# Two-layer transformer block: five of 21 pairs of score maxima per block as halves of 256 keys, in a new order of sixteen key tiles

## The chip, the cores and the metric

The kernel runs on one core of one Trainium2 chip. The metric is the device time of one execution in microseconds. Before the change it is 3515.99 us, the median of three runs (3515.44 to 3516.27).

## The reference

Two rounds of the same pair of layers: attention with 32 heads of 20 elements over 2048 positions, then a dense layer with a squared ReLU. All of it is float32.

```
qkv = (x @ wqkv).reshape(B, S, 3, H, Dh)...      # B=1, S=2048, D=640, H=32, Dh=20
scores = einsum("bhqd,bhkd->bhqk", q, k) * Dh ** -0.5
o = einsum("bhqk,bhkd->bhqd", softmax(scores), v) ... @ wo
...
x = x + A(layernorm(x));  x = x + B(layernorm(x))      # B: relu(x @ w1 + b1)**2 @ w2 + b2
x = x + A(layernorm(x));  x = x + B(layernorm(x))      # the same weights again
```

The softmax subtracts the maximum of each row of scores, so the kernel needs each row's maximum over all 2048 keys before it may compute an exponential.

## The kernel before, in words

Each layer is a projection stage (queries, keys, values), an attention sweep, and the dense layer. The change is in the sweep.

**Blocks.** A block is four heads (a group g of eight) and 512 queries (one of four). There are 32 blocks per layer. The four heads lie as two pairs p; within a pair the even head's operands are on partitions 0 to 59 or 61 and the odd head's on partitions 64 and up. A product of an even head uses the upper half of TensorE's rows, one of an odd head the lower half, so one of each can run at the same time. I call these the two lanes.

**One key tile** (128 keys) of a block takes three kinds of work:

- `score` (L795 before, L832 after): keys by queries, 128x512 into one PSUM bank, four per key tile (two pairs, two heads). ScalarE takes the exponential (`exps`, L805 before, L842 after) into a tile e.
- `pv` (L810 before, L847 after): the value step, e times the values of four heads, added up in bank 7 over sixteen key tiles. It uses all rows of the array.
- `smax` (L701 for the product, L712 for the reduction before; L715 and L726 after): queries by keys, 128 queries by 512 keys of one head into one bank, and a VectorE reduction to one maximum per query. This is for a block that comes up later; the maxima of a block go into one small tile mx, from which `mrows_max` makes the negative maxima that are loaded as two further rows of the queries.

**What sets the order.** The program is written out by hand: `attention` runs through the string ORDER_OF_BLOCK over and over, and `op` issues what a letter stands for. One pass over the string is sixteen key tiles. `a` and `b` are the next score of the even and of the odd head with its exponential, `S` is both at once in two neighbouring banks with one exponential of 1024 columns, `m` and `n` are a whole maximum of the even and of the odd head, and `V` is the value step. The letters between two V are one run of products. When all maxima are done, LAST_ORDER takes over, which the change leaves alone.

**Banks.** Seven of the eight PSUM banks serve scores and maxima. The class Clock keeps a model of the engines while the program is written and gives each product the bank that its model says is free first. Its numbers decide which bank a product takes, and so which earlier reader it waits for; they take no part in the run.

**Waits.** A matmul is a weight load and a product on TensorE; a wait stands on the weight load. Completions of TensorE's matmuls are counted in one count. Where a matmul has to wait for another of TensorE's own, the kernel puts a step (`nc.tensor.nop`) on TensorE's queue that waits for that count, and makes the matmul wait for the step. Today this is in `Halves.catch` (L406), in the projections, where the matmul waited for is nineteen back.

Of the kernel before, what the change touches and what calls it, by code (L numbers as in the profile page):

```python
# [16 lines left out]
P = 128  # L17
# [8 lines left out]
QB = 512  # L26
# [15 lines left out]
def tile_layers(  # L42
# [22 lines left out]
    def name(p):  # L65
        n_alloc[0] += 1
        return f"{p}{n_alloc[0]}"
# [506 lines left out]
    class Clock:  # L574


        def __init__(self):
            self.free = [600 * ((b - ps_q.n - 1) % 5 - 5) for b in range(5)] + [0, 0]
            self.lane, self.over, self.fresh, self.place = [0, 0], [0, 0], [False, False], 9
            self.now, self.load, self.values, self.since = 0, 0, False, 0  # L580
            self.act, self.act_end, self.dve = 0, 0, 0
            self.ready, self.used, self.acc = {}, [], 0

        def row(self, par, b):
            s = self.now + 3
            if self.values:
                s = self.now + 542
                self.values, self.fresh, self.place = False, [True, True], 0
                self.lane, self.over, self.since = [0, 0], [0, 0], None
            s = max(s, self.lane[par], self.load)  # L590
            w = max(s - 116, self.free[b] + 34)
            t = max(s, w + 61)
            more = max(0, w + 116 - t)
            if self.since is None:
                self.since = t
            self.now = t
            self.load = 0 if w + 177 < t else w + 116 + (46 if t > s + 10 else 0)
            self.lane[par] = t + 232 + more
            if self.fresh[par]:
                self.fresh[par] = False  # L600
                self.lane[par] = max(self.lane[par], self.since + 338)
            self.over[par] = t + more
            self.place += 1
            return t + more + {1: 532, 2: 563, 3: 465}.get(self.place, 433)

        def first(self):
            return min(range(7), key=self.free.__getitem__)

        def score(self, par, kt):
            b = self.first()  # L610
# [7 lines left out]
            return banks[:, b, :]  # L618

        def both(self, kt):  # L620
            b = min(range(6), key=lambda b: max(self.free[b : b + 2]))
# [87 lines left out]
    def smax(dst, t, p, sub, c, par):  # L709

        by_queries(dst, t, p, sub, c, par)
        nc.vector.tensor_reduce(  # L712
            maxima(t)[:, 2 * p + par, sub, c : c + 1], dst, axis=AX.X, op=ALU.max
        )

    def pair_of(t, p, sub, c):
# [6 lines left out]
    def smax_two(t, p, sub, c):  # L723

        for par, dst in enumerate(pair_of(t, p, sub, c)):
            nc.vector.tensor_reduce(  # L726
                maxima(t)[:, 2 * p + par, sub, c : c + 1], dst, axis=AX.X, op=ALU.max
            )

    def step_two(t, p, sub, x):  # L730
# [6 lines left out]
    def both_two(t, p, sub, x, r):  # L737

        c = 2 * "de".index(x)
        for par, dst in enumerate(pair_of(t, p, sub, c)):  # L740
            nc.vector.tensor_tensor_reduce(  # L741
                out=r[par],
                in0=dst,
                in1=r[par],
                scale=1.0,
                scalar=LEAST,
                op0=ALU.add,
                op1=ALU.max,
                accum_out=maxima(t)[:, 2 * p + par, sub, c : c + 1],
            )  # L750

    PAIRS = [(p, sub) for p in range(2) for sub in range(4)]
# [161 lines left out]
        [(0, 0, "d"), (0, 1, "d")],  # L914
        [(1, 0, "d"), (1, 1, "d"), (2, 0, "d"), (2, 1, "d")],
    ]
    PARTLY = {g * NQB + qb for x in DOUBLE for g, qb, c in x}

# [27 lines left out]
    def qkv(first, x_src, rest, lead):  # L946
# [204 lines left out]
    def attention(first, x_src, first_rows):  # L1151
# [1 line left out]
        es_of = {}  # L1153
        e_n.clear()
        weights.extend(slot([P, 2, QB], F32, "e") for _ in range(6))
        st_n, sm_n = [0, 0], [0, 0]
        state = {"begun": -1, "done": 0, "acc": None, "debt": 0}
        clock = Clock()
        todo = [
# [13 lines left out]
        ends = {x[0]: n for n, x in enumerate(todo)}  # L1173
        blocks = sorted(ends)
        firsts = {todo[0][0]: 0, **{t: ends[s] + 1 for s, t in zip(blocks, blocks[1:])}}
        over = {t for t in range(NBLK) if t not in ends and t not in done}
        rows = {"next": min(t for t in range(NBLK) if t not in done), "at": None}

        def begin(i):
# [27 lines left out]
            if i in split:  # L1207
                split.pop(i)()

        def op(o):  # L1210
            if o in "abS":
                pars = (0, 1) if o == "S" else ("ab".index(o),)
                i, p = divmod(st_n[pars[0]], 2)
                assert len(pars) == 1 or st_n[0] == st_n[1]
                if i >= last:
                    return
                if i > state["begun"]:
                    state["begun"] = i
                    begin(i)
                es = es_of.setdefault(i, {})  # L1220
                dst = clock.both(i) if o == "S" else clock.score(pars[0], i)
                for par in pars:
                    st_n[par] += 1
                    score(
                        dst[:, par, :] if o == "S" else dst,
                        i // NKT, i % NKT, 2 * p + par, es,
                    )
                exps(es[p] if o == "S" else es[p][:, pars[0], :], dst)
            elif o in "mn":
                par = "mn".index(o)  # L1230
                n = sm_n[par]
                if n == len(todo):
                    return
                t, p, sub, c = todo[n]
                if n == firsts[t] and par == 0:
                    for s in blocks[blocks.index(t) :][:2]:
                        if s not in q_t:
                            load_q(s)
                if (t // NQB, c) not in k_t or t not in q_t:
                    return  # L1240
                sm_n[par] += 1
                smax(clock.most(par), t, p, sub, c, par)
                if n == ends[t] and min(sm_n) > n:
                    over.add(t)
                    if t * NKT > state["begun"] + 2 * NKT:
                        del q_t[t]
# [24 lines left out]
            op(o)  # L1271
            yield
        while state["done"] < last:
            for o in LAST_ORDER if min(sm_n) == len(todo) else ORDER_OF_BLOCK:
                op(o)
        assert min(sm_n) == len(todo)
        q_t.clear()
        k_t.clear()
        v_t.clear()
# [451 lines left out]
```

## Time and profile before

| | |
|---|---|
| median of three runs | 3515.99 us |
| profiled execution, its own time | 3517.9 us |
| its span from first to last instruction | 3516.1 us |
| TensorE busy | 3504.1 us |
| ScalarE (ACT) busy | 2733.7 us |
| VectorE (DVE) busy | 2732.5 us |
| granted TensorE clock | 0.999 |

The page gives busy time per engine; PE is TensorE's products, PEld its weight loads, which run beside products. Ends of matmuls are modelled, so their starts carry more than their lengths. The groups of instructions give busy time and mean duration of one, then the idle time before them and who ended it.

### The profile page before, as it was taken

What the parts mean: (1) busy time and instruction counts of PE and PEld (TensorE: products, weight loads), DVE (VectorE), ACT (ScalarE), POOL (GpSimd) and SP (SyncE); (2) the same over time, 40 slices, a digit from 0 to 9 for tenths busy, and PEclk for the clock granted to TensorE, in tenths of its full rate; (3) what the DMA queues carried; (4) which work ended last, traced back from release to release, by engine and by line L of the source; (5) the groups of instructions that cost most, each with busy time, mean ns of one, the idle gap of its engine ahead of it and who ended that gap; (6) DMA issues with size and microseconds to landing.
All of it is one profiled execution on the core that took longest, in us unless ns stands there. A gap on an engine that the chain in (4) does not pass through costs nothing.

```text
span 3516.1 us, 71077 instructions
## 1 busy us (share of the span) xinstructions
PE 3504.1 (100%) x25292; PEld 2112.9 (60%) x25292; DVE 2732.5 (78%) x5326; ACT 2733.7 (78%) x4804; POOL 828.0 (24%) x975
## 2 busy tenths in 40 slices
PE   9999999999999999999999999999999999999999
PEld 8998333333333335989989983333333333358899
DVE  8999888888888882566869988888888888825667
ACT  5888999999999996123348889999999999951233
POOL 4430334443112111120143201121221212111200
PEclk9999999999999999999999999999999999999999
DMA  7766454444222135856656652222222121358574
GB/s 259 234 207 188 143 170 134 135 126 133 60 55 60 42 103 192 310 198 237 234 195 224 194 180 69 77 76 57 77 76 55 53 58 50 103 196 308 195 253 141
DMA packets 325378, 514.87 MB, mean 146 GB/s; under 512 B 74532, under 2 KB 149796, under 8 KB 325024
## 3 DMA queue, kind: packets, MB, share of 16 engines
q1 hardware_dynamic: 324496, 508.62, 45.5%
q8 instruction: 201, 3.29, 0.4%
q10 hardware_dynamic: 528, 1.70, 0.2%
q14 instruction: 153, 1.25, 0.1%
HBM read 326.95 MB, written 183.21 MB: 145 GB/s over the span
## 4 chain that ended last, share of the span: by engine, by line
PE 96%; DMA 2%; ACT 1%; POOL 0%; DVE 0%; issue 0%; SPq 0%; POOLq 0%; ACTq 0%; DVEq 0%
PE banks L810 28%; PE banks L795 18%; PE banks L701 18%; PE banks L376 13%; PE banks L1455 9%; PE banks L396 6%; PE banks L408 5%; PE banks L391 0%; PE banks L508 0%; ACT e L805 0%; DMA x<-d_x 0%; DMA x<-in_A_x_dram 0%; SPq L78 0%; DMA few<-d_s 0%; DMA o<-d_r 0%
## 5 line engine op out<-in xcount | busy, mean ns | idle before, releaser
L805 ACT ACTIVATE e<-banks 128x512 f32<-128x512 f32 (+1 forms) x3416 | 2035.1, 691 | 56.3 <-PE banks L795 21.5
L712 DVE TENSOR_REDUCE mx<-banks 128x1 f32<-128x512 f32 x2560 | 1620.3, 685 | 321.6 <-PE banks L701 274.4
L810 PE MATMUL banks<-e,vg 128*32 128x512 f32 x8192 | 1093.5, 605 | 2.2 <-ACT e L805 2.1
L701 PE MATMUL banks<-k,q 60*128 60x512 f32 x3360 | 1060.1, 411 | 0.9 <-DMA q<-d_qk 0.9
L795 PE MATMUL banks<-q,k 62*128 62x512 f32 x4096 | 1049.0, 441 | 1.2 <-ACT v L472 0.6
L795 PEld LDWEIGHTS banks<-q,k 62*128 62x128 f32 x4096 | 514.6, 184 | 748.5 <-ACT e L805 440.9
L701 PEld LDWEIGHTS banks<-k,q 60*128 60x128 f32 x3360 | 568.0, 185 | 196.4 <-ACT e L805 64.2
L741 DVE CUSTOM_DVE_ANT_0 rl<-banks,rl 128x512 f32<-128x512 f32 x736 | 477.0, 689 | 31.1 <-PE banks L701 6.7
L734 ACT ACTIVATE rl<-banks 128x512 f32<-128x512 f32 x736 | 399.7, 602 | 57.0 <-PE banks L701 46.5
L810 PEld LDWEIGHTS banks<-e,vg 128*32 128x32 f32 x8192 | 162.2, 108 | 353.5 <-issue 270.6
L408 PE MATMUL banks<-xnT,wqk 64*128 64x512 f32 x1080 | 327.7, 393 | 0.0
L376 PE MATMUL banks<-xnT,w 128*128 128x512 f32 x1440 | 327.0, 389 | 0.0
L396 PE MATMUL banks<-xnT,wqk 64*128 64x512 f32 x1080 | 326.9, 395 | 0.0
L376 PEld LDWEIGHTS banks<-xnT,w 128*128 128x128 f32 x1440 | 270.2, 188 | 56.0
L1361 ACT ACTIVATE r<-banks,b_t 128x512 f32<-128x512 f32 x96 | 66.2, 690 | 222.1 <-PE banks L376 205.1
L854 POOL TENSOR_TENSOR few<-few,minus_t 128x16 f32<-128x16 f32 x62 | 179.9, 2902 | 239.4 <-DMA few<-d_s 234.4
L701 PE MATMUL banks<-kd,q 60*128 60x512 f32 x736 | 210.1, 398 | 0.8 <-ACT rl L734 0.6
L408 PEld LDWEIGHTS banks<-xnT,wqk 64*128 64x128 f32 x1080 | 202.1, 188 | 8.5
L396 PEld LDWEIGHTS banks<-xnT,wqk 64*128 64x128 f32 x1080 | 200.3, 187 | 11.1 <-issue 1.7
L865 POOL TENSOR_TENSOR o<-o 128x512 f32<-128x512 f32 x62 | 79.6, 1284 | 508.6 <-DMA o<-d_r 285.5
L308 POOL CAST mr<-nt 128x32 fp32r<-128x32 f32 x64 | 13.5, 212 | 775.9 <-DVE nt L767 775.9
L396 PE MATMUL banks<-wv,xnT 64*128 64x320 f32 x960 | 193.5, 308 | 0.0
(130 smaller groups left out, 3295.5 us busy)
## 6 DMA issues: line engine op xcount, KB each, us to landing
q<-d_qk SPq DMA_DIRECT2D x876, 80.0 KB
d_qk<-ev SPq DMA_DIRECT2D x80, 512.0 KB
k<-d_qk SPq DMA_DIRECT2D x444, 80.0 KB
x<-d_x SPq DMA_DIRECT2D x96, 320.0 KB
w<-d_w SPq DMA_DIRECT2D x60, 480.0 KB
d_h<-r SPq DMA_DIRECT2D x48, 512.0 KB
r<-d_h SPq DMA_DIRECT2D x48, 512.0 KB
d_o<-ot SPq DMA_DIRECT2D x248, 80.0 KB
```

The source lines that it names most:

```text
L376: nc.tensor.matmul(dst, a, b, start=(n == 0), stop=(n == last))
L396: top = nc.tensor.matmul(dst, a[:64], b[:64], start=start, stop=last)
L408: low = nc.tensor.matmul(dst, a, b, start=False, stop=last, skip_group_check=True)
L701: nc.tensor.matmul(dst, q_t[t][b : b + 60, p, sub * P : (sub + 1) * P], k_t[t // NQB, c][b : b + 60, p, :], start=True, stop=True,)
L712: nc.vector.tensor_reduce(maxima(t)[:, 2 * p + par, sub, c : c + 1], dst, axis=AX.X, op=ALU.max)
L734: nc.scalar.activation(r, dst, AF.Relu)
L741: nc.vector.tensor_tensor_reduce(out=r[par], in0=dst, in1=r[par], scale=1.0, scalar=LEAST, op0=ALU.add, op1=ALU.max, accum_out=maxima(t)[: ...
L795: nc.tensor.matmul(dst, k_t[t // NQB, kt // 4][b : b + 62, p, (kt % 4) * P : (kt % 4 + 1) * P], q_t[t][b : b + 62, p, :], start=True, stop ...
L805: nc.scalar.activation(dst, src, AF.Exp, scale=SCALE)
L810: nc.tensor.matmul(acc[32 * h : 32 * h + 32, :], v_t[t // NQB, kt // 8][:, kt % 8, 32 * h : 32 * h + 32], es[p][:, par, :], start=(kt == 0 ...
L854: nc.gpsimd.tensor_tensor(few, few, minus_t, op=ALU.pow)
L1455: nc.tensor.matmul(dst, a, b, start=first and not more, stop=last, skip_group_check=more)
```

## The change

Five of the 21 pairs of maxima in a pass are taken as halves. A pair is a block's 128 queries and 512 keys for the even and the odd head of a pair p: before, two whole products into two banks and two reductions. In halves it is taken twice, each time 256 keys for both heads: the first product (`h` for the even head first, `i` for the odd head first) opens a bank and fills one half of its columns, and later `j` fills the other half with the other head. Then one VectorE reduction (`most_of_halves`, L746) takes both maxima from that bank. So five pairs are twenty products of 256 keys and ten reductions in place of ten products of 512 keys and ten reductions. Between `h` or `i` and `j` stands a step on TensorE's queue that waits for the first half, because both write one bank from different lanes.

The string of letters is new: ten openings by `h` or `i`, each with its `j`, one more `S` with one `a` and one `b` fewer, and another order. The runs, between two `V`:

```
before: (m)bbanna bamnabm nabmnab Snanbm nambabm Sbmna Snabm SnSm bmamnS bmanban anabmbm bambann bmabanm Smban Snabm SnSm
after:  bhanmjS Sbmna SnSm bhmnajba bhmnajab hbmnajab ainmbjS SnmS ainabjmb aibSjan mbmbna bhmnajba bhmnajab nhabajmb Smban SSnm
```

Each mx tile holds eight maxima per query where it held four (a slot for each half), and is set to the least number before it is used. The list of maxima to take is shared by whole and half pairs (`taken`), and a block is done when all of its products are counted (`less`).

```diff
+        def row(self, par, b, cut=0, after=0):
+            s = max(self.now + 3, after)
...
-            self.lane[par] = t + 232 + more
+            self.lane[par] = t + 232 + more - cut
...
+        def half(self, par):
+            self.opened = self.first()
+            self.later = self.row(par, self.opened, 106) + 110
+            return banks[:, self.opened, :]
+
+        def other(self, par):
+            b = self.opened
+            t = max(self.row(par, b, 106, self.later), self.dve)
+            self.opened = None
+            self.dve, self.free[b] = t + 610, t + 698
...
-            mx_t[t] = small.tile([P, 4, 4, 4], F32, tag="mx", bufs=14, name=name("mx"))
-            if t in PARTLY:
-                nc.vector.memset(mx_t[t], LEAST)
+            mx_t[t] = small.tile([P, 4, 4, 8], F32, tag="mx", bufs=14, name=name("mx"))
+            nc.vector.memset(mx_t[t], LEAST)
...
+    def half_scores(dst, t, p, sub, c, half, par):
+
+        b = 64 * par
+        w = QB // 2
+        return nc.tensor.matmul(
+            dst[:, par * w : (par + 1) * w],
+            q_t[t][b : b + 60, p, sub * P : (sub + 1) * P],
+            k_t[t // NQB, c][b : b + 60, p, half * w : (half + 1) * w],
+            start=True,
+            stop=True,
+            skip_group_check=True,
+        )
+
+    def most_of_halves(dst, t, p, sub, c, half):
+
+        n = 2 * c + half
+        nc.vector.tensor_reduce(
+            maxima(t)[:, 2 * p : 2 * p + 2, sub, n : n + 1],
+            dst.rearrange("p (a c) -> p a c", a=2),
+            axis=AX.X,
+            op=ALU.max,
         )
...
     ORDER_OF_BLOCK = (
-        "bbannaVbamnabmVnabmnabVSnanbmVnambabmVSbmnaVSnabmVSnSmVbmamnSVbmanbanVan"
-        "abmbmVbambannVbmabanmVSmbanVSnabmVSnSmVm"
+        "bhanmjSVSbmnaVSnSmVbhmnajbaVbhmnajabVhbmnajabVainmbjSVSnmSVai"
+        "nabjmbVaibSjanVmbmbnaVbhmnajbaVbhmnajabVnhabajmbVSmbanVSSnmV"
     )
...
+            elif o in "hi":
+                if not parted:
+                    x = taken()
+                    if x is None:
+                        return
+                    parted.extend([(*x, 0), (*x, 1)])
+                x, par = parted.pop(0), "hi".index(o)
+                dst = clock.half(par)
+                opened.append((x, par, dst, half_scores(dst, *x, par)))
+            elif o == "j":
+                if not opened:
+                    return
+                x, par, dst, one = opened.pop()
+                clock.other(1 - par)
+                step = nc.tensor.nop()
+                tc.add_manual_dep(step.ins, one.ins.name, SYNC)
+                two = half_scores(dst, *x, 1 - par)
+                tc.add_manual_dep(two.ins, step.ins.name, SYNC)
+                most_of_halves(dst, *x)
+                less(x[0])
```

Two places on TensorE's queue show what moves. The first is a run of seven products in the sweep, before the change: L701 is a whole maximum, L795 a score, L810 the value step that closes the run. DVE and Activation in brackets are the readers that have to leave a bank first.

```order
L701 MATMUL banks<-k_1180,q_12667 128x512
L795 MATMUL banks<-q_12530,k_5404 128x512 [waits DVE_49]
L795 MATMUL banks<-q_12530,k_5404 128x512 [waits Activation_49]
L795 MATMUL banks<-q_12530,k_5404 128x512
L701 MATMUL banks<-k_1180,q_12667 128x512 [waits DVE_49]
L701 MATMUL banks<-k_1180,q_12667 128x512 [waits Activation_49]
L795 MATMUL banks<-q_12530,k_5404 128x512
L810 MATMUL banks<-e_5359,vg_11921 32x512 [waits DVE_49]
```

In letters this is mbbanna: three products of even heads and four of odd heads, none of which waits for another of TensorE's own.

A run of the changed kernel in the sweep, bhmnajba; L832 is a score, L715 a whole maximum, L734 a half, L847 the value step.

```order
L832 MATMUL banks<-q_14290,k_5516 128x512
L734 MATMUL banks<-k_4970,q_14087 128x256 [waits DVE_49]
L715 MATMUL banks<-k_4979,q_14087 128x512 [waits Activation_49]
L715 MATMUL banks<-k_4979,q_14087 128x512
L832 MATMUL banks<-q_14290,k_5516 128x512 [waits DVE_49]
L734 MATMUL banks<-k_4970,q_14087 128x256 [waits PE_49,PE_sequencer_49]
L832 MATMUL banks<-q_14290,k_5516 128x512 [waits Activation_49]
L832 MATMUL banks<-q_14290,k_5516 128x512
L847 MATMUL banks<-e_5355,vg_13645 32x512 x2
```

Each lane now has three whole products and one half. The second half waits for TensorE's own count (PE) through the step on its queue (PE_sequencer), three products after the first half, and two whole products stand behind it. The first half has a whole product ahead of it.

The second place is the one run of a pass, hbmnajab, in which the half stands ahead of everything else.

```order
L734 MATMUL banks<-k_4979,q_14087 128x256 [waits Activation_49]
L832 MATMUL banks<-q_14290,k_5516 128x512 [waits DVE_49]
L715 MATMUL banks<-k_4979,q_14087 128x512 [waits Activation_49]
L715 MATMUL banks<-k_4979,q_14087 128x512 [waits DVE_49]
L832 MATMUL banks<-q_14290,k_5516 128x512 [waits Activation_49]
L734 MATMUL banks<-k_4979,q_14087 128x256 [waits PE_49,PE_sequencer_49]
L832 MATMUL banks<-q_14290,k_5516 128x512 [waits DVE_49]
```

Here the first half is the run's first product, and four products stand between it and the second half.

More of the change, by code (lines that the diff above doesn't have):

```diff
@@ L582, in __init__ @@
             self.ready, self.used, self.acc = {}, [], 0
-        def row(self, par, b):
-            s = self.now + 3
+            self.opened, self.later = None, 0
+        def row(self, par, b, cut=0, after=0):
+            s = max(self.now + 3, after)
             if self.values:
-                s = self.now + 542
+                s = max(self.now + 542, after)
                 self.values, self.fresh, self.place = False, [True, True], 0
@@ L597, in row @@
             self.load = 0 if w + 177 < t else w + 116 + (46 if t > s + 10 else 0)
-            self.lane[par] = t + 232 + more
+            self.lane[par] = t + 232 + more - cut
             if self.fresh[par]:
                 self.fresh[par] = False
-                self.lane[par] = max(self.lane[par], self.since + 338)
+                self.lane[par] = max(self.lane[par], self.since + 338 - cut)
             self.over[par] = t + more
             self.place += 1
-            return t + more + {1: 532, 2: 563, 3: 465}.get(self.place, 433)
+            return t + more + {1: 532, 2: 563, 3: 465}.get(self.place, 433) - cut
         def first(self):
-            return min(range(7), key=self.free.__getitem__)
+            return min((b for b in range(7) if b != self.opened), key=self.free.__getitem__)
         def score(self, par, kt):
@@ L620, in both @@
         def both(self, kt):
-            b = min(range(6), key=lambda b: max(self.free[b : b + 2]))
+            b = min(
+                (b for b in range(6) if self.opened not in (b, b + 1)),
+                key=lambda b: max(self.free[b : b + 2]),
+            )
             t = max(self.row(par, b + par) for par in range(2))
@@ L712, in smax @@
         nc.vector.tensor_reduce(
-            maxima(t)[:, 2 * p + par, sub, c : c + 1], dst, axis=AX.X, op=ALU.max
+            maxima(t)[:, 2 * p + par, sub, 2 * c : 2 * c + 1], dst, axis=AX.X, op=ALU.max
+        )
+    def half_scores(dst, t, p, sub, c, half, par):
[8 more added lines that the diff above has]
+            skip_group_check=True,
+        )
+    def most_of_halves(dst, t, p, sub, c, half):
[5 more added lines that the diff above has]
+            op=ALU.max,
         )
@@ L726, in smax_two @@
             nc.vector.tensor_reduce(
-                maxima(t)[:, 2 * p + par, sub, c : c + 1], dst, axis=AX.X, op=ALU.max
+                maxima(t)[:, 2 * p + par, sub, 2 * c : 2 * c + 1], dst, axis=AX.X, op=ALU.max
             )
@@ L748, in both_two @@
                 op1=ALU.max,
-                accum_out=maxima(t)[:, 2 * p + par, sub, c : c + 1],
+                accum_out=maxima(t)[:, 2 * p + par, sub, 2 * c : 2 * c + 1],
             )
@@ L1155, in attention @@
         weights.extend(slot([P, 2, QB], F32, "e") for _ in range(6))
-        st_n, sm_n = [0, 0], [0, 0]
+        st_n = [0, 0]
+        whole, sm_n, parted, opened = [], [0, 0], [], []
         state = {"begun": -1, "done": 0, "acc": None, "debt": 0}
@@ L1172, in attention @@
             loads[at] = lambda qb=qb: heads(nc.sync, qb, 4)
[L1173 to L1176, printed above, removed]
+        todo.reverse()
+        undone = {}
+        for x in todo:
+            undone[x[0]] = undone.get(x[0], 0) + 2
+        blocks, begun = sorted(undone), set()
+        over = {t for t in range(NBLK) if t not in undone and t not in done}
         rows = {"next": min(t for t in range(NBLK) if t not in done), "at": None}
@@ L1208, in begin, with taken, less @@
                 split.pop(i)()
+        def taken():
+            if not todo:
+                return None
+            t, p, sub, c = todo[-1]
+            if t not in begun:
+                begun.add(t)
+                for s in blocks[blocks.index(t) :][:2]:
+                    if s not in q_t:
+                        load_q(s)
+            if (t // NQB, c) not in k_t or t not in q_t:
+                return None
+            return todo.pop()
+        def less(t):
+            undone[t] -= 1
+            if undone[t] == 0:
+                over.add(t)
+                if t * NKT > state["begun"] + 2 * NKT:
+                    del q_t[t]
         def op(o):
@@ L1230, in op @@
                 par = "mn".index(o)
[L1231 to L1240, printed above, removed]
+                if sm_n[par] == len(whole):
+                    x = taken()
+                    if x is None:
+                        return
+                    whole.append(x)
+                t, p, sub, c = whole[sm_n[par]]
                 sm_n[par] += 1
                 smax(clock.most(par), t, p, sub, c, par)
[L1243 to L1246, printed above, removed]
+                less(t)
+            elif o in "hi":
+                if not parted:
+                    x = taken()
+                    if x is None:
+                        return
[5 more added lines that the diff above has]
+                if not opened:
+                    return
+                x, par, dst, one = opened.pop()
[6 more added lines that the diff above has]
+                less(x[0])
             else:
@@ L1273, in attention @@
         while state["done"] < last:
-            for o in LAST_ORDER if min(sm_n) == len(todo) else ORDER_OF_BLOCK:
+            for o in LAST_ORDER if not any(undone.values()) else ORDER_OF_BLOCK:
                 op(o)
-        assert min(sm_n) == len(todo)
+        assert not any(undone.values())
         q_t.clear()
```

1 line of the change is left out of this document (removed).

## The prediction

> **What bounds the kernel now.** I read the page first: the busy shares, then the chain that ended last, then the costliest groups. TensorE is busy through the whole span, and the chain is 96% TensorE; the three lines of the attention sweep (L810 values, L795 scores, L701 maxima) make 64% of it.
>
> ```profile
> span 3516.1 us, 71077 instructions
> PE 3504.1 (100%) x25292; PEld 2112.9 (60%) x25292; DVE 2732.5 (78%) x5326; ACT 2733.7 (78%) x4804; POOL 828.0 (24%) x975
> ...
> PE 96%; DMA 2%; ACT 1%; POOL 0%; DVE 0%; issue 0%; SPq 0%; POOLq 0%; ACTq 0%; DVEq 0%
> ...
> L712 DVE TENSOR_REDUCE mx<-banks 128x1 f32<-128x512 f32 x2560 | 1620.3, 685 | 321.6 <-PE banks L701 274.4
> L810 PE MATMUL banks<-e,vg 128*32 128x512 f32 x8192 | 1093.5, 605 | 2.2 <-ACT e L805 2.1
> L701 PE MATMUL banks<-k,q 60*128 60x512 f32 x3360 | 1060.1, 411 | 0.9 <-DMA q<-d_qk 0.9
> L795 PE MATMUL banks<-q,k 62*128 62x512 f32 x4096 | 1049.0, 441 | 1.2 <-ACT v L472 0.6
> ```
>
> A busy TensorE alone does not say that less work on it saves time, so I looked at one pass over sixteen key tiles in the table by stretches (columns: length, then busy time and instructions of PE, PEld, DVE, ACT, POOL, clock, DMA share, GB/s).
>
> ```profile
> 706.23:738.97 32.74, 32.74 (x238) 12.54 (x235) 27.54 (x46) 31.87 (x55) 15.60 (x20) 1.00 0.50 143
> ```
>
> ACT is busy 31.87 of 32.74 us, so it is the next bound, close behind. But the waits of the engine PE name it with 2.1 us in the whole span: today ACT follows TensorE.
>
> ```profile
> PE banks L810 <- ACT e L805: 2.1, 5, 0.7
> ```
>
> The timeline of engine PE shows how a tile's time is made. Here are a tile of six products and one of seven (start, duration, line, count); L810 is the value step that ends each run.
>
> ```profile
> 704.33 0.72 PE L795 MATMUL banks<-q,k 62*128 62x512 f32 x3
> 704.67 0.61 PE L701 MATMUL banks<-k,q 60*128 60x512 f32 x2
> 704.91 0.40 PE L795 MATMUL banks<-q,k 62*128 62x512 f32 x1
> 705.23 1.06 PE L810 MATMUL banks<-e,vg 128*32 128x512 f32 x8
> ...
> 707.38 1.06 PE L810 MATMUL banks<-e,vg 128*32 128x512 f32 x8
> 708.38 0.50 PE L795 MATMUL banks<-q,k 62*128 62x512 f32 x1
> 708.38 0.72 PE L701 MATMUL banks<-k,q 60*128 60x512 f32 x2
> 708.72 0.65 PE L795 MATMUL banks<-q,k 62*128 62x512 f32 x3
> 709.19 0.40 PE L701 MATMUL banks<-k,q 60*128 60x512 f32 x1
> 709.52 1.06 PE L810 MATMUL banks<-e,vg 128*32 128x512 f32 x8
> ```
>
> From the first product to the next value step six products take 0.90 us (704.33 to 705.23) and seven take 1.14 (708.38 to 709.52); the value step adds 1.00 before the next run (707.38 to 708.38). Even and odd heads lie on different partitions, and two products, one of each, run side by side. I call the even heads' partitions one lane and the odd heads' the other. Six products are three per lane; seven are four and three. A lane takes a new product every 0.23 us (704.67 with x2 lasts 0.61, a single one 0.39 or so: the second began 0.22 to 0.23 later), and the seventh costs a full 0.24 while one lane stands idle. The value step starts 0.32 to 0.33 after the last product's start (704.91 to 705.23).
>
> **The change part by part.** A pass keeps 42 maxima and 64 products of scores: ten runs of seven and six of six. By the maxima's row there are 2560 / 42 = 61 passes with maxima in both layers together. The change splits five pairs per pass into halves, so that each of the ten runs of seven becomes 3.5 and 3.5. If halves were free, such a run would end midway between 0.90 and 1.14, at 1.02: 0.12 saved, times 10 times 61, **73 us**. That is the gross gain.
>
> What it adds stands in the run itself. The first half (call it h) and the second (j) write one bank from different lanes, so j waits for h through a step on TensorE's queue, and the queue is in order: behind j stand the run's last two products, one of which shares j's lane. I work out when j can start, from the run's first product as zero.
>
> First, the end of h. In nine of the ten runs h stands second, beside a whole product of the other lane that began first. The queue waits on one count for all of TensorE's matmuls, so that count reaches h's number only when the whole product before it has also ended: 0.50 after the run's start (708.38 lasts 0.50). h alone would end earlier; the groups by form give its length from products of 512 and 320 columns.
>
> ```profile
> L408 PE MATMUL banks<-xnT,wqk 64*128 64x512 f32 x1080 | 327.7, 393 | 0.0
> ...
> L408 PE MATMUL banks<-wv,xnT 64*128 64x320 f32 x960 | 190.4, 306 | 0.0
> ```
>
> 393 less 306 ns over 192 columns is 0.45 ns a column, so 256 columns fewer are 0.11 us: h alone ends at 0.39, and a half holds its lane for 0.23 less 0.11, 0.12 us.
>
> Second, from there to j's weight load: a signal to the queue, the step, and a signal to the load. The step exists in today's kernel at L406, where it never holds anything up; the two signals I take from a place where TensorE waits late in a run, which also gives the third term.
>
> ```profile
> L406 PEldq EVENT_SEMAPHORE  x136: 51/51/51, 33.1 to 2078.3; - x136
> ```
>
> ```profile
> 509.52 1.03 ACT L805 ACTIVATE e<-banks 128x1024 f32<-128x1024 f32 x1
> 509.88 0.73 PE L701 MATMUL banks<-k,q 60*128 60x512 f32 x2
> 510.44 1.29 DVE L712 TENSOR_REDUCE mx<-banks 128x1 f32<-128x512 f32 x2 [0.40 <-PE banks L701]
> 510.61 0.19 PEld L795 LDWEIGHTS banks<-q,k 62*128 62x128 f32 x2 [0.20 <-ACT e L805]
> 510.61 0.49 PE L795 MATMUL banks<-q,k 62*128 62x512 f32 x2
> 511.04 0.16 PEld L810 LDWEIGHTS banks<-e,vg 128*32 128x32 f32 x8 [0.24 <-issue]
> ```
>
> ACT ended at 510.55 and the waiting load began at 510.61: 0.06 for a signal. A product that began at 509.88 with its weights not yet there lasts 0.50, so it ended at 510.38, and DVE started at 510.44: 0.06 again. So 0.06 + 0.05 + 0.06 = 0.17, and j's load starts at 0.50 + 0.17 = 0.67. Third, a load that waits is no longer hidden: the product at 510.61 lasts 0.49 where others last 0.39, so j streams 0.10 later, from 0.77. Then 0.12 for j's lane, the whole product behind it at 0.89, and the value step 0.32 after that: **1.21 against 1.14, 0.07 lost** per run, where 0.12 was to be won. Without the wait, j would have begun at 0.57 (a product with an exposed load, 0.34 as from 708.38 to 708.72, then 0.23), which hardly leaves room: the work ahead of j hides the wait up to 0.57, and 0.20 of it stays in sight.
>
> In the tenth run the half stands first in the queue, and its count depends on nothing beside it: 0.39 + 0.17 + 0.10 + 0.12 + 0.32 = 1.10, 0.04 won. A pass loses 9 x 0.07 less 0.04, 0.59 us; 61 passes lose **36 us**.
>
> The rest I cost at nothing. Maxima are still 42 reductions of 128x512 elements a pass, and DVE is busy 27.54 of 32.74 us; the larger tile of maxima costs a longer last reduction and a memset per block, below 1 us each, off the path while DVE has those 5 us of slack. ACT gets 53 operations for 55 and a longer pass. If that cover went, DVE would have to lose 5 us a pass before it showed. SP issues as many DMAs as before, some of them a few places earlier or later because they hang on a key tile or a block's last maximum; in the groups above TensorE waits 0.9 us for one transfer in the whole span, so a shift of that size has no price.
>
> Bounds of the unknown wait. From below: it is hidden wholly (1.02, 73 us won). With h's own end as release in all ten runs it is 1.10, 24 us won. From above: a further signal of 0.06 in each run, because the last product waits for a bank that the delayed reduction frees late, gives 0.06 x 10 x 61 = 37 us more, 73 lost. I take 36, since the three terms have rows at hand, and the count of the other product is how the queue is written.
>
> The Trainium skill ("TensorE: Matmul & The Clock Gate", part 3 on packing small matmuls) says that matmuls end strictly in program order and that each counted one adds about 26 ns behind the other. By that h's count would come some 0.03 after its neighbour's 0.50, and the estimate would be 9 x 0.10 less 0.04, times 61, 52 us lost. No row here shows the counts.
>
> Against the profiled execution's own time, 3517.9 us (1.8 around the span), this is 3554; the median of the runs, 3515.99, lies 1.9 lower, so I predict **3552 us**.
>
> **The rivals.** First, the plan works: the wait lies wholly behind the other lane's products. For it speaks that j would otherwise start only at 0.57; against it the 0.17 of signals and the 0.10 of an exposed load, which the rows show separately. 73 us gained gives 3443; as ACT cannot do a pass in much less than its 31.87 us, it may stop near 3452. Chance 13%. Second, the wait bites in part: either h's own end releases it, or j's weights are loaded ahead so that the 0.10 falls away (0.67 + 0.12 + 0.32 = 1.11). Both give 0.03 to 0.04 won in each run, about 3494. Against the second form stands 510.61, where the load itself waited. Chance 13%. The same page of the Trainium skill, in part 2, has weight loads pulled ahead of matmuls in flight, which is that second form; the row at 510.61 does not bear it out for a load with a wait of its own. Third, gain and loss cancel: with signals of 0.03 the runs end at 1.15 and the tenth at 1.04, no change, 3516. Chance 8%. Fourth, late banks on top of the wait: the delayed reduction frees its bank after the order of banks counted on it, another 0.06 a run, 3589. For it speaks that seven banks serve everything; against it, that DVE reaches j's reduction only after at least one whole maximum of the same run in nine of ten. Chance 10%. That the change does not do what it says is excluded: halves, waits and order stand in the built program.
>
> **How the numbers follow.** My forecast, 3530 to 3575, has 56%. The range for 8 in 10 leaves out the first rival and about half of the fourth: 3478 to 3580. A measurement here tells some 0.2% (7 us) from no change. Faster by more: the first two rivals, 0.26. Within: the third, 0.08. Slower: my case and the fourth, 0.66.
>
> **What would show it.** In the changed kernel's timeline a run with halves would last about 1.2 us from its first product to the value step, with j's weight load at 0.64 to 0.70 after the run's start and j itself lasting about 0.39 (a half with its load exposed) where h's neighbours show the same 0.10. Runs of six should stay at 0.90. ACT's share of a pass would fall. If the runs with halves last 1.02 to 1.10, the wait is hidden or shorter than the rows say and the forecast is wrong; if j starts as I say but runs last longer, look for waits on DVE or ACT at the last two products.

## The result: 54 us slower

The changed kernel takes 3569.77 us, the median of four runs (3569.3 to 3572.32), against 3515.72 before (3514.76 to 3516.27). The ratio is 1.0156, with a 95% interval of 1.0138 to 1.0173: 54 us, 1.6%. The forecast was 3552 us, slower, with a range of 3478 to 3580.

The page of the changed kernel, in the lines that answer to those of before:

```profile
span 3568.3 us, 73162 instructions
PE 3554.2 (100%) x25904; PEld 2126.1 (60%) x25904; DVE 2739.6 (77%) x5366; ACT 2730.5 (77%) x4742; POOL 827.2 (23%) x975
...
L832 PE MATMUL banks<-q,k 62*128 62x512 f32 x4096 | 1128.3, 437 | 2.2 <-DVE mx L726 0.5
L847 PE MATMUL banks<-e,vg 128*32 128x512 f32 x8192 | 1092.2, 605 | 2.6 <-ACT e L842 2.4
...
L715 PE MATMUL banks<-k,q 60*128 60x512 f32 x2748 | 806.1, 405 | 0.0
...
L734 PE MATMUL banks<-k,q 60*128 60x256 f32 x1224 | 465.1, 380 | 0.7 <-ACT v L472 0.3
L746 DVE TENSOR_REDUCE mx<-banks 128x2 f32<-128x512 f32 x612 | 418.6, 684 | 50.8 <-PE banks L734 50.8
```

TensorE is as busy as before, and longer; DVE and ACT are busy for the same time as before, to 0.3%. A reduction of two halves (L746, 684 ns) costs what a whole one does (685 before). A half of 256 columns lasts 380 ns where whole products last 405 to 437: that is the first sign that halves run with their weight loads in sight (256 columns fewer were to be 0.11 us less, about 0.28).

One pass over sixteen key tiles, in the table by stretches:

```profile
646.60:680.05 33.45, 33.45 (x248) 12.77 (x244) 27.48 (x46) 31.76 (x55) 14.81 (x20) 1.00 0.35 115
```

It takes 33.45 us against 32.74, and ACT's share falls from 97% to 95% (31.76 of 33.45). The two sweeps last, from their first to their last value step, 1065.5 and 1064.3 us against 1039.0 and 1039.6: 51 of the 52 us by which the span grew lie in them.

The run bhmnajba from that pass, in the timeline, products first (PE), then weight loads (PEld):

```profile
646.60 0.50 PE L832 MATMUL banks<-q,k 62*128 62x512 f32 x1
646.60 0.38 PE L734 MATMUL banks<-k,q 60*128 60x256 f32 x1
646.82 0.50 PE L715 MATMUL banks<-k,q 60*128 60x512 f32 x2
647.06 0.40 PE L832 MATMUL banks<-q,k 62*128 62x512 f32 x1
647.28 0.38 PE L734 MATMUL banks<-k,q 60*128 60x256 f32 x1
647.29 0.60 PE L832 MATMUL banks<-q,k 62*128 62x512 f32 x2
647.82 0.64 PE L847 MATMUL banks<-e,vg 128*32 128x512 f32 x4
```

```profile
646.83 0.19 PEld L832 LDWEIGHTS banks<-q,k 62*128 62x128 f32 x1
647.28 0.18 PEld L734 LDWEIGHTS banks<-k,q 60*128 60x128 f32 x1 [0.27 <-PEq L1313]
647.28 0.29 PEld L832 LDWEIGHTS banks<-q,k 62*128 62x128 f32 x2
647.82 0.16 PEld L847 LDWEIGHTS banks<-e,vg 128*32 128x32 f32 x8 [0.25 <-issue]
```

The second half's load starts 0.68 us after the run's first product, and what it waited for is named: the step at L1313 on TensorE's queue. The two products behind it load behind it too (647.28, x2). The value step follows at 1.22. The view of that step says who waited for it in the whole span (us, times; idle times below 0.15 us are not listed):

```profile
L1313 PEldq EVENT_SEMAPHORE  x612: 51/51/51, 330.8 to 3133.4; - x153
...
  PEld banks L734: 129.1, 486
```

Mean run lengths in ns by place in the pass, worked out for 58 passes of each trace from the start of a run's first product to the start of its value step (before has other letters at the same places; its means are 1124 to 1163 for the ten runs of seven and 899 to 903 for the six of six). The columns belong to the changed kernel and to four of the experiments below, with the letters of the change:

```
place      change   half first  second last  whole maxima  two steps
bhanmjS     1224       1145        1250          1159         1388
Sbmna        911        912         911           934          900
SnSm         965        911         908           897          975
bhmnajba    1224       1115        1211          1138         1384
bhmnajab    1231       1082        1070          1142         1383
hbmnajab    1083       1077        1142          1137         1237
ainmbjS     1236       1662        1145          1598         1386
SnmS         895        903         910           894          905
ainabjmb    1227       1111        1254          1164         1383
aibSjan     1235       1102        1131          1135         1392
mbmbna       906       1008        1114           901          906
bhmnajba    1229       1080        1023          1141         1381
bhmnajab    1228       1077        1182          1139         1384
nhabajmb    1231       1084        1035          1128         1394
Smban        901        903         903           909          901
SSnm         898        905         925           902          899
```

In the change, nine of the ten runs with halves last 1.22 to 1.24 us and the tenth, in which the half stands first, 1.08.

### The profile page after: what moved, and what is told of

It is laid out like the page before. It is cut to its first block, busy times and chain, and to the rows that moved or that the text cites. A ratio compares the mean times of both kernels' runs of the same rounds, so it can differ in the third digit from the quotient of the medians.

```text
span 3568.3 us, 73162 instructions
## 1 busy us (share of the span) xinstructions
PE 3554.2 (100%) x25904; PEld 2126.1 (60%) x25904; DVE 2739.6 (77%) x5366; ACT 2730.5 (77%) x4742; POOL 827.2 (23%) x975
## 4 chain that ended last, share of the span: by engine, by line
PE 93%; DMA 3%; POOL 1%; SPq 1%; DVE 1%; issue 1%; ACT 0%; POOLq 0%; ACTq 0%; DVEq 0%
PE banks L847 26%; PE banks L832 17%; PE banks L715 14%; PE banks L376 12%; PE banks L1527 8%; PE banks L396 6%; PE banks L408 4%; PE banks L734 4%; SPq L78 1%; PE banks L391 1%; DMA x<-d_x 1%; DMA raw<-in_B_w_dram 0%; PE banks L508 0%; DMA few<-d_s 0%; DVE bst L284 0%
## 5 line engine op out<-in xcount | busy, mean ns | idle before, releaser
L726 DVE TENSOR_REDUCE mx<-banks 128x1 f32<-128x512 f32 x1948 | 1264.2, 686 | 318.1 <-PE banks L715 266.0
L832 PE MATMUL banks<-q,k 62*128 62x512 f32 x4096 | 1128.3, 437 | 2.2 <-DVE mx L726 0.5
L847 PE MATMUL banks<-e,vg 128*32 128x512 f32 x8192 | 1092.2, 605 | 2.6 <-ACT e L842 2.4
L832 PEld LDWEIGHTS banks<-q,k 62*128 62x128 f32 x4096 | 553.7, 185 | 721.9 <-ACT e L842 387.7
L715 PE MATMUL banks<-k,q 60*128 60x512 f32 x2748 | 806.1, 405 | 0.0
L715 PEld LDWEIGHTS banks<-k,q 60*128 60x128 f32 x2748 | 393.8, 185 | 127.0 <-ACT e L842 101.2
L734 PE MATMUL banks<-k,q 60*128 60x256 f32 x1224 | 465.1, 380 | 0.7 <-ACT v L472 0.3
L746 DVE TENSOR_REDUCE mx<-banks 128x2 f32<-128x512 f32 x612 | 418.6, 684 | 50.8 <-PE banks L734 50.8
L734 PEld LDWEIGHTS banks<-k,q 60*128 60x128 f32 x1224 | 223.7, 183 | 192.6 <-PEq L1313 129.1
L847 PEld LDWEIGHTS banks<-e,vg 128*32 128x32 f32 x8192 | 161.7, 108 | 296.3 <-issue 246.3
L715 PE MATMUL banks<-kd,q 60*128 60x512 f32 x736 | 207.1, 398 | 0.7 <-ACT rl L771 0.6
```

What stands on the lines that cost most here:

```text
L715: nc.tensor.matmul(dst, q_t[t][b : b + 60, p, sub * P : (sub + 1) * P], k_t[t // NQB, c][b : b + 60, p, :], start=True, stop=True,)
L726: nc.vector.tensor_reduce(maxima(t)[:, 2 * p + par, sub, 2 * c : 2 * c + 1], dst, axis=AX.X, op=ALU.max)
L734: return nc.tensor.matmul(dst[:, par * w : (par + 1) * w], q_t[t][b : b + 60, p, sub * P : (sub + 1) * P], k_t[t // NQB, c][b : b + 60, p, ...
L746: nc.vector.tensor_reduce(maxima(t)[:, 2 * p : 2 * p + 2, sub, n : n + 1], dst.rearrange("p (a c) -> p a c", a=2), axis=AX.X, op=ALU.max,)
L832: nc.tensor.matmul(dst, k_t[t // NQB, kt // 4][b : b + 62, p, (kt % 4) * P : (kt % 4 + 1) * P], q_t[t][b : b + 62, p, :], start=True, stop ...
L847: nc.tensor.matmul(acc[32 * h : 32 * h + 32, :], v_t[t // NQB, kt // 8][:, kt % 8, 32 * h : 32 * h + 32], es[p][:, par, :], start=(kt == 0 ...
```

## The experiments

All were timed beside the kernel before on the same chip. The theory is that the wait for the first half sets the length of the runs: released by TensorE's count, then a step, a signal and an exposed load. The rivals are that halves cost by themselves, and that the new order of key tiles does.

**Two banks.** The halves go into neighbouring banks, and nothing on TensorE waits for TensorE.

```diff
-            return banks[:, self.opened, :]
+            return banks[:, b : b + 2, : QB // 2]
...
-                step = nc.tensor.nop()
-                tc.add_manual_dep(step.ins, one.ins.name, SYNC)
-                two = half_scores(dst, *x, 1 - par)
-                tc.add_manual_dep(two.ins, step.ins.name, SYNC)
+                half_scores(dst, *x, 1 - par)
```

> The change, but the two halves go into two neighbouring banks and one reduction reads both, so the second half needs no wait; order and number of products as in the change. If the loss is the wait on TensorE's queue, a run of seven should last about 1.02 us from its first product to the value step (1.22 in the changed kernel), 0.12 below the 1.14 of before in 610 runs: 3443 us, or up to 3460 where ACT holds it back. If the halves themselves cost (more matmuls, more weight loads, the reduction of two halves), it stays near 3570. If the extra bank is what is short, runs wait on DVE and it lands between.

3875.45 us, ratio 1.1024 (1.1008 to 1.1041). The third branch named the cause, a bank short, but not its size, nor that most of the waits are for ACT. A run bhmnajba in its timeline of weight loads (L835 a score, L737 a half, L718 a whole maximum, L850 the value step):

```profile
606.71 0.18 PEld L737 LDWEIGHTS banks<-k,q 60*128 60x128 f32 x1
606.82 0.28 PEld L718 LDWEIGHTS banks<-k,q 60*128 60x128 f32 x2
607.41 0.18 PEld L835 LDWEIGHTS banks<-q,k 62*128 62x128 f32 x1 [0.32 <-ACT e L845]
607.41 0.18 PEld L737 LDWEIGHTS banks<-k,q 60*128 60x128 f32 x1
607.52 0.19 PEld L835 LDWEIGHTS banks<-q,k 62*128 62x128 f32 x1
607.95 0.18 PEld L835 LDWEIGHTS banks<-q,k 62*128 62x128 f32 x1 [0.24 <-ACT e L845]
608.37 0.16 PEld L850 LDWEIGHTS banks<-e,vg 128*32 128x32 f32 x8 [0.24 <-issue]
```

The second half's load (607.41) now follows the score ahead of it at once, so its wait is gone. But two scores wait for a bank that ACT still reads, idle 0.32 and 0.24 us, and the run lasts 1.66 where by subtraction it would be near 1.1 without them. In the change a run takes seven banks (six whole products and one bank of two halves), here it takes eight. That banks were short, and not only badly chosen, can be followed in the trace, since the program fixes which bank each product takes: over 58 passes, in eight of the ten places none of the seven banks is free while the run's last product waits; in the other two a pair of scores waits, which needs two neighbouring banks, and no two neighbours are free. The wait's price cannot be read from this run.

**The half first.** In all ten runs the first half is moved ahead of the whole product beside it.

```diff
-        "bhanmjSVSbmnaVSnSmVbhmnajbaVbhmnajabVhbmnajabVainmbjSVSnmSVai"
-        "nabjmbVaibSjanVmbmbnaVbhmnajbaVbhmnajabVnhabajmbVSmbanVSSnmV"
+        "hbanmjSVSbmnaVSnSmVhbmnajbaVhbmnajabVhbmnajabVianmbjSVSnmSVi"
+        "anabjmbViabSjanVmbmbnaVhbmnajbaVhbmnajabVhnabajmbVSmbanVSSnmV"
```

> The change, with the first half moved to the very start of each of the ten runs (it stood second in nine); the same bank and the same wait. If TensorE's one count makes the wait last until the whole product ahead of the half has ended, the step on the queue now starts at 0.43 us of the run instead of 0.57, the second half's load at 0.53 instead of 0.68, and a run lasts 1.09 us: 0.05 below the kernel before in 610 runs, about 3488 us. If the wait is the same wherever the half stands, it stays at 3565 to 3575.

3538.01 us, ratio 1.0064 (1.0049 to 1.0079): 32 us better than the change, but not 3488. Nine of the ten places are 1.08 to 1.15, where the theory has 1.09; one, ianmbjS, is 1.66, and a run of six, mbmbna, 1.01. Both kinds in the timeline of weight loads, hbmnajab and ianmbjS:

```profile
671.03 0.18 PEld L734 LDWEIGHTS banks<-k,q 60*128 60x128 f32 x1 [0.84 <-ACT e L842]
...
671.57 0.18 PEld L734 LDWEIGHTS banks<-k,q 60*128 60x128 f32 x1
671.57 0.29 PEld L832 LDWEIGHTS banks<-q,k 62*128 62x128 f32 x2
672.11 0.16 PEld L847 LDWEIGHTS banks<-e,vg 128*32 128x32 f32 x8 [0.24 <-issue]
673.10 0.18 PEld L734 LDWEIGHTS banks<-k,q 60*128 60x128 f32 x1 [0.84 <-ACT e L842]
...
673.63 0.18 PEld L734 LDWEIGHTS banks<-k,q 60*128 60x128 f32 x1
674.35 0.19 PEld L832 LDWEIGHTS banks<-q,k 62*128 62x128 f32 x2 [0.54 <-ACT e L842]
674.79 0.16 PEld L847 LDWEIGHTS banks<-e,vg 128*32 128x32 f32 x8 [0.25 <-issue]
```

The second half's load starts 0.53 to 0.54 after the first in both, where it was 0.68 in the change: the place of the half in the queue is worth 0.15 us. What lengthens ianmbjS comes after it: the pair of scores waits 0.54 for its banks, which ACT still reads. (By the banks in the program, two of the seven are free meanwhile, but no two neighbours, as the pair needs.) Those two places cost 1.66 less 1.08 and 1.01 less 0.90, 0.69 us a pass or 42 us in 61 passes; without them it would be about 3496, an estimate from these rows.

**The second half last.** It is moved to the end of its run, so that its lane has other work while it waits.

```diff
-        "bhanmjSVSbmnaVSnSmVbhmnajbaVbhmnajabVhbmnajabVainmbjSVSnmSVai"
-        "nabjmbVaibSjanVmbmbnaVbhmnajbaVbhmnajabVnhabajmbVSmbanVSSnmV"
+        "bhanmSjVSbmnaVSnSmVbhmnabajVbhmnaabjVhbmnaabjVainmbSjVSnmSVa"
+        "inabmbjVaibSanjVmbmbnaVbhmnabajVbhmnaabjVnhabambjVSmbanVSSnmV"
```

> The change, with the second half moved to the end of its run, just before the value step: two whole products fewer stand behind it, and its lane is busy until 0.8 us. The wait itself is unchanged, its step still starts at 0.57 us of the run, but by then the lane has work left, so it should cost nothing: runs of 1.02 us, about 3443 us, up to 3460 if ACT holds it back. If the halves cost by themselves, or the wait blocks TensorE's queue whatever stands behind it, it stays above 3540.

3540.59 us, ratio 1.0073 (1.0058 to 1.0088). That is just on the side of the rival ("above 3540"), but the runs say otherwise. Where nothing else is in the way the wait is hidden wholly, as in nhabambj (timeline, PE):

```profile
655.36 0.49 PE L715 MATMUL banks<-k,q 60*128 60x512 f32 x1
655.37 0.38 PE L734 MATMUL banks<-k,q 60*128 60x256 f32 x1
655.59 0.74 PE L832 MATMUL banks<-q,k 62*128 62x512 f32 x4
656.05 0.39 PE L715 MATMUL banks<-k,q 60*128 60x512 f32 x1
656.17 0.28 PE L734 MATMUL banks<-k,q 60*128 60x256 f32 x1
656.38 0.64 PE L847 MATMUL banks<-e,vg 128*32 128x512 f32 x4
```

1.02 us, and the second half lasts 0.28 instead of 0.38: its load lay beside other work. It lasts 0.28 in all ten places (medians of 58 passes), so its own wait costs nothing any more. But only two of the ten do as well as this run (1023 and 1035 in the table); the rest are 1.07 to 1.25, and mbmbna grows to 1.11. In their weight loads it is whole products that wait for a bank, as in the first bhmnabaj, in mbmbna and in the second bhmnaabj:

```profile
634.91 0.19 PEld L832 LDWEIGHTS banks<-q,k 62*128 62x128 f32 x2 [0.26 <-ACT e L842]
...
649.51 0.19 PEld L832 LDWEIGHTS banks<-q,k 62*128 62x128 f32 x2 [0.16 <-DVE mx L746]
...
653.77 0.23 PEld L832 LDWEIGHTS banks<-q,k 62*128 62x128 f32 x2 [0.17 <-DVE mx L746]
```

The first waits for ACT. The other two wait for L746, the reduction of two halves: a bank that was filled late is wanted again before it has been read. Seven of the eight slower places have a wait of 0.13 to 0.30 us for a bank (means of 58 passes), the first bhmnaabj (1.07) hardly any. How much of each loss these waits make was not worked out.

**Whole maxima in the new order.** The halves are taken out and the order is kept as far as it goes. The larger mx tile and its first setting stay, so their cost is tested along with the order.

```diff
-        "bhanmjSVSbmnaVSnSmVbhmnajbaVbhmnajabVhbmnajabVainmbjSVSnmSVai"
-        "nabjmbVaibSjanVmbmbnaVbhmnajbaVbhmnajabVnhabajmbVSmbanVSSnmV"
+        "bmanmSVSbmnaVSnSmVbmnanbaVbmnamabVbmnanabVanmbmSVSnmSVanabnm"
+        "bVabSmanVmbmbnaVbmnanbaVbmnamabVnabanmbVSmbanVSSnmV"
```

> The new order of sixteen key tiles with whole maxima in place of the halves: each of the ten runs of seven has four products in one lane and three in the other again. If the order of tiles by itself is neutral, runs of seven last 1.14 us and it takes 3516 us, give or take 10. If the new order costs by itself (scores and exponentials further apart, five exponentials in one run), it takes 3530 or more.

3550.37 us, ratio 1.0099 (1.0082 to 1.0116). Nine of the ten runs are 1.13 to 1.16, no worse than before; one, anmbmS, is 1.60:

```profile
676.36 0.18 PEld L832 LDWEIGHTS banks<-q,k 62*128 62x128 f32 x1
676.97 0.18 PEld L832 LDWEIGHTS banks<-q,k 62*128 62x128 f32 x1 [0.42 <-ACT e L842]
677.39 0.16 PEld L847 LDWEIGHTS banks<-e,vg 128*32 128x32 f32 x8 [0.24 <-issue]
```

The second score of an S waits 0.42 for its bank, at the same place as with the half first. 1.60 less 1.14 is 0.46, times 61, 28 of the 36 us. By the time alone the second branch came true, the order costs; by the runs that cost is nearly all one bank that comes late, and elsewhere the order is neutral. In the change itself this place does not stall (1.24), so this cost is not part of its 54 us. That its longer runs give the banks time would explain that, but is not shown.

**Two steps.** The wait is lengthened: a second step between the halves, which waits for the first.

```diff
-                step = nc.tensor.nop()
-                tc.add_manual_dep(step.ins, one.ins.name, SYNC)
+                first = nc.tensor.nop()
+                tc.add_manual_dep(first.ins, one.ins.name, SYNC)
+                step = nc.tensor.nop()
+                tc.add_manual_dep(step.ins, first.ins.name, SYNC)
```

> The changed kernel with two steps in a row on TensorE's queue between the halves, the second waiting for the first; nothing else is different. If the wait of the second half sets the end of the run, its whole price is on the path: one more step and one more signal, 0.105 us (from the step's start to the weight load behind it is 0.106 us in the changed kernel), in all ten runs of 61 passes, 64 us more: about 3634. If the runs are held by something else (banks, ACT, the halves themselves), part of it hides and it takes 3570 to 3600.

3664.41 us, 95 above the change. A run bhmnajba in its timeline of weight loads:

```profile
671.88 0.18 PEld L734 LDWEIGHTS banks<-k,q 60*128 60x128 f32 x1
...
672.71 0.18 PEld L734 LDWEIGHTS banks<-k,q 60*128 60x128 f32 x1 [0.42 <-PEq L1315]
672.72 0.29 PEld L832 LDWEIGHTS banks<-q,k 62*128 62x128 f32 x2
673.25 0.16 PEld L847 LDWEIGHTS banks<-e,vg 128*32 128x32 f32 x8 [0.24 <-issue]
```

The load is at 0.83 and the value step at 1.37, each 0.15 later than with one step. All ten places grew by 0.15 to 0.16, so 0.155 x 10 x 61, 95 us, is the whole difference: the wait lies on the path in every run, none of it hidden. A second step with its signal costs 0.155 on the queue, not the 0.105 I had put in.

**An order searched with the wait as measured.** Halves as in the change; the order and the choice of banks are new. The model that gives out the banks is corrected (release in program order, load 0.106 behind the step, a late load exposed), and the letters are searched with it.

```diff
-            return t + more + {1: 532, 2: 563, 3: 465}.get(self.place, 433) - cut
+            told = t + more + {1: 532, 2: 563, 3: 465}.get(self.place, 433)
+            self.told = max(self.told + 34, told - 106 if half else told)
+            return told - 106 if half else told
...
-            self.later = self.row(par, self.opened, 106) + 110
+            self.row(par, self.opened, True); self.later = self.told + 106
...
+        "hbnamjSVSabmnVSbmnaVmbhnabajVbhmbanajVhbmnajabVainmbSjVSnmSV"
+        "ianabjbmViabSjanVnambmbVbmhnabajVhbmnabajVhnabmjabVabmbanVSmnSV"
```

> Halves as in the change, in an order that was searched with the kernel's own model of the engines (it chooses the banks) after its rule for the second half was set to what the changed kernel's trace shows: the step is released by the count in program order (0.034 after the product ahead), the weight load follows 0.106 later, and a waiting load is not hidden. Six of the ten runs open with the half, in four the second half is late in the run; no run should stall on a bank for long. If the wait and the seven banks are all that costs, a pass is about 0.3 us below the one of before and 61 passes give 3498 us, between 3490 and 3508. If halves cost by themselves, it does not come below 3516.

3507.57 us in eleven runs against 3514.59: ratio 0.9980 (0.9971 to 0.9989), 7 us faster than before the change and at the upper end of the range expected. One pass is

```profile
656.75:689.19 32.44, 32.44 (x249) 13.57 (x245) 27.67 (x47) 31.93 (x56) 19.69 (x25) 1.00 0.37 115
```

with ACT busy 31.93 of 32.44 us. The mean of 58 passes is 32.52 us against 32.73 before, 0.22 gained where 0.3 was expected. Its ten runs with halves average 1025 to 1186 ns, bhmbanaj 1027. So halves need not cost anything, and the loss of the change is a matter of where they stand. How much of the 7 us is due to the halves and how much to the search is not parted: whole maxima in an order searched anew were not timed.

## Why the prediction was right, and where its size was off

**The mechanism held, and one agreement was luck.** The second half was forecast to load at 0.64 to 0.70: it loads at 0.68. It was to last about 0.39 with its load exposed: it lasts 0.38. Runs with halves were to last 1.21: they last 1.22 to 1.24. The run with the half in front was to be 1.10: it is 1.08. ACT's share fell. That the wait is what makes the runs long is shown by the second step (all of its price on the path), by moving the half forward (load at 0.53, runs of 1.08) and by hiding the wait (runs of 1.02).

Inside the wait, though, two errors nearly cancel. I had the release at the end of the whole product beside the half (0.50) and 0.17 from there to the load. The trace also keeps the moments at which TensorE's count rises; here are medians of 58 passes in the nine places. The whole product is counted at 0.510 to 0.514 us of the run. The half would end at 0.385 by its own length, but it is counted 0.034 behind the whole product, at 0.544 to 0.548, whichever of the two lanes it is in. The step starts 0.028 after that and the load 0.106 after the step's start: 0.134. So the release was 0.045 later and the way to the load 0.035 shorter than in my sum, and that 0.67 met 0.68 is luck. In the tenth place the half is counted 0.014 after its own end (0.398), and the load follows at 0.53, not 0.56.

The Trainium skill ("TensorE: Matmul & The Clock Gate", part 3 on packing small matmuls) says that matmuls end in program order and that each counted one adds about 26 ns; by it the prediction estimated a loss of 52 us. The trace agrees with the order and has 34 ns for the 26. That 52 came nearer to 54 than my 36 is in part chance: that estimate had the load at 0.50 + 0.03 + 0.17 = 0.70.

**The size: 54 against 36.** The terms are in the table of runs. The length before was right (1.139 on average for 1.14), but the nine runs average 1.229 and not 1.21: 0.09 lost in each where I had 0.07, 11 us more in 61 passes. The tenth won 0.06 instead of 0.04, 1 us less. Together the ten runs are 0.755 us a pass longer (12148 ns in sum against 11393), not 0.59. The runs of six were taken as unchanged, but together grew by 0.07 us, nearly all of it at SnSm (0.965), 4 us; why was not traced. 0.755 and 0.07 times 61 are 50 us; the rest lies outside the passes.

**The gross gain** of 0.12 a run is real, as single runs of 1.02 in two experiments show. No form had it in all ten runs: each of the three that shorten or hide the wait (two banks, the half first, the second half last) ran into the seven banks. Nor could all of the 73 us be had: they are 1.2 us a pass, and 32.74 less 1.2 is below the 31.87 us that ACT is busy. My fourth rival named late banks as an extra on top of the wait. In the change they hardly count, but they are the next bound behind it, and I had not priced them in the experiments' expectations: four of six missed for that reason (3443 for 3875 and for 3541, 3488 for 3538, 3516 for 3550). A fifth, 3634 for 3664, took a step for 0.105 that costs 0.155.

**The rivals.** The first (the wait is hidden) falls by the row at 647.28. The second falls in both forms for nine runs: h's own end does not release it where a whole product is ahead, and the load was not pulled ahead of its own wait. In the tenth run, with the half in front, its first form is what happened, as forecast. The third was half right: with signals of 0.03 it had 0.11 from the release to the load, and 0.134 is nearer to that than to my 0.17. It fails because the release itself came later. The fourth falls with the time.

**Open.** Whether halves in two banks could win in an order made for them was not tried. How near the searched order is to the best one is not known; ACT's 31.93 us of a 32.44 us pass leaves little.

## What to carry to other kernels

When a product on one half of the array waits for one on the other, count the whole path: here the count of TensorE's products told of the first one only after the longer product issued ahead of it, then came the step, the signal, and a weight load that no longer hid. Put the product that others wait for first in the queue, and the waiting one where its lane still has work. And ask what is held meanwhile: here a bank opened early, so that curing the wait exposed the banks, and of the forms tried only an order that weighed both beat the kernel before, by 0.2%.

## What the runs showed that I had not expected

A second step on TensorE's queue that waits for the first adds 0.155 us, though the step itself is 51 ns long. The other surprise is how close the seven banks are to their limit: an eighth bank per run with halves cost each of them about 0.4 us or more (1.66 against 1.22 in the run shown), and shifting one product by one place cost a run 0.4 us, at one place of sixteen (1.24 in the change, 1.66 with the half first).
